# Twelve output products in two bursts of six, and a higher limit for fourth blocks, in a two-sided attention kernel

## The chip, the cores and the metric

The kernel runs on one core of a Trainium2 chip. The metric is the device time of one execution in microseconds; the kernel before takes 1789.94 us, the median of three runs (1789.69 to 1790.98).

## What is computed

Two attention layers read the same input x (2048 x 512) and are mixed row by row. Side A is full softmax attention with 32 heads of 16; side B is softmax attention inside four segments of 512 rows, with a mask, plus a linear memory of the earlier segments. Cut to what matters:

```
a = softmax(q k^T / 4) v, over all 2048 keys, heads joined, @ a_wo
b = per segment: g * (phi(q) M) / (phi(q) z) + (1 - g) * softmax(q k^T / 4 + mask) v, @ b_wo
    M, z: running sums of phi(k) v and phi(k) over the segments before
out = gate * a + (1 - gate) * b,   gate = sigmoid(sum(x * gate_w))
```

## The kernel before

A first phase projects x to q, k and v of both sides and stores them in HBM; it also runs the first 96 row-maximum products. Then comes the main loop, lines 993 to 1025, in which the order of the work is written out by hand: one pass is a slot n, 2368 of them.

A **unit** is a side, a group of four heads and a segment of 512 query rows: 32 units of side A with 64 slots each, 32 of side B with 10. They alternate A, B, A, B (line 102), so a pair takes 74 slots. In one slot the kernel issues

- a score product (`score_part`, line 707): keys by queries into one of three PSUM banks `st`; ACT takes the exponential into a buffer `p` (L745, or L742 for two half pieces of side B). Four slots fill one `p` tile; six such tiles exist (`NP`), and line 716 asserts that the oldest one waiting is still among them. For side B, GpSimd then zeroes the part above the diagonal (L726);
- a row-maximum product for the slot 96 further on (`max_part`, line 214, called with `m = n + LEAD`): queries by keys into one of four PSUM banks `sm`, in rotation, which DVE reduces to one maximum per row (L226 for side A; for side B the masked reduction L238, on one or two parts of the bank). Score and maximum products use the two halves of the rows of the array.

After every third slot (`BURST = 3`) follows one **burst** on PE. It is either P @ V work or work from the list `shared`:

- `some_values` (line 757) takes blocks of 128 keys from `queue` and adds their product with v into the single PSUM bank `ops`; blocks that lie side by side in one `p` tile go into one set of four matmuls, one for each head, at four column positions. How many blocks a burst takes is set by `most` (line 984): three (`MOST`), and a fourth where the queue is longer than a limit that falls from `HIGH` at the unit's first block to `LOW` at its last; near a unit's end the table `ends` (line 982) sets the number. For side B the limit is `LOW` throughout;
- when the last block of a unit is done, ACT copies `ops` to SBUF (L782) and it goes to HBM (L783). From then on the twelve products of `output` (line 911) may be due: half of the products of a block of 128 rows of an earlier segment, the attention of four groups of heads as high and low parts times the output weights, added up in `ops`; ACT copies the sum out (`keep`, L929, or `leave`, L933). The dictionary `between` (lines 942 to 944) says after which units of side A this happens: those of the segments 1 to 3 but for the last two. After the units of side A of segment 0 the twelve products of `later_tile` (line 639) follow in the same way; they are projections of q that the first phase left out;
- while `shared` has anything, a burst takes four pieces of it, so the twelve products fill three bursts, and P @ V waits for that long.

In the last 96 slots (`wide`, line 702) there are no maximum products left; bursts come after six slots and take up to eight blocks. The octets (line 813) scale the raw results on GpSimd at set numbers of slots after a unit's end. DMAs are issued by SP.

Of the kernel before, what the change touches and what calls it, by code (L numbers as in the profile page):

```python
# [26 lines left out]
NO = 4  # L27
# [8 lines left out]
BURST = 3  # L36
LATER = (2, 3)
MOST = 3
LOW, HIGH = 6, 14
NP = 6  # L40
GAP = {"A": 2, "B": 5}
LATE_T = 9
# [5 lines left out]
def gated_mix(ctx, tc, x, xT, wqkv, a_wo, b_wq, b_wk, b_wv, b_wo, beta, gate_w, out):  # L48
# [88 lines left out]
    def raw(t):  # L137

        return t[:].bitcast(F32)
# [109 lines left out]
    def run_todo(m):  # L249

        for e in [e for e in todo if e[0] <= m]:
            todo.remove(e)
            e[1]()
# [359 lines left out]
    def load_halves(key, tag, src, os, n, ns):  # L613

        k = {}

        def load():
            if os[0] == 0:
                halved[key] = wo.tile([128, NO, 2, D], F32R, tag=tag, name="w" + tag)
            if len(os) == 2:  # L620
                t = fr.tile([128, 2, 2, 2, 128], F32R, tag="blk", name="wraws", bufs=2)
                k["t"] = raw(t).rearrange("p k o h t -> p k (o h t)")
            else:
                k["t"] = fr.tile([128, D], F32, tag="res", name="wraw", bufs=2).unsqueeze(1)
            nc.sync.dma_start(k["t"], src[128 * os[0]:128 * os[-1] + 128].rearrange("(k p) d -> p k d", p=128))

        def split(i, o):
            h = halved[key][:, o]
            nc.gpsimd.tensor_copy(h[:, 0], k["t"][:, i])
            nc.gpsimd.tensor_sub(h[:, 1], k["t"][:, i], h[:, 0].bitcast(F32))  # L630
            ready.add((key, o))
        at(n, load)
        for i, o in enumerate(os):
            at(ns[i], lambda i=i, o=o: split(i, o))

    def x_later(c):
        return xT[:, c * CH:(c + 1) * CH]

    def later_tile(c, o):

        def done():
            full = fr.tile([128, CH], F32, tag="part", name="full")
            nc.scalar.copy(full, ops)
            t = fr.tile([128, 2, 2, 2, 128], F32R, tag="blk", name="qhalves", bufs=2)
            t = t.rearrange("p a o h t -> p a (o h t)")
            nc.gpsimd.tensor_copy(t[:, 0], full)
            nc.gpsimd.tensor_sub(t[:, 1], full, t[:, 0].bitcast(F32))
            for i in range(2):
                at(n + 12, lambda i=i: nc.sync.dma_start(
                    qd["A", o, c][16 * i:16 * i + 16].rearrange("d h t -> (d h) t"), raw(t[:, i])))  # L650


            if o == NO - 1 and c == LATER[0]:
                for i in range(2):
                    load_halves(("x", LATER[1]), "B", x_later(LATER[1]), (2 * i, 2 * i + 1), n + 2 + 18 * i,
                                [n + 24 + 29 * i, n + 28 + 29 * i])
            elif o == NO - 1:
                for i, (side, w) in enumerate((("A", a_wo), ("B", b_wo))):
                    load_halves(side, side, w, (0, 1), n + 2 + 18 * i, [n + 22 + 8 * i, n + 26 + 8 * i])
                    for k in range(2, 4):  # L660
                        load_halves(side, side, w, (k,), n + 50 + 22 * i + 3 * (k - 2), [n + 62 + 18 * i + 5 * (k - 2)])

        def f(i):
            k, (a, b) = i // 3, ((1, 0), (0, 1), (0, 0))[i % 3]
            assert {("q", k), (("x", c), k)} <= ready
            nc.tensor.matmul(ops, halved["q"][:, k, a, o * 128:(o + 1) * 128], halved["x", c][:, k, b],  # L666
                             start=(i == 0), stop=(i == 11))
            if i == 11:
                done()
        for i in range(12):  # L670
            yield lambda i=i: f(i)
# [85 lines left out]
    def some_values(n, most):  # L757

        while queue and most and queue[0][0] <= n:
            _, u, i = queue.pop(0)  # L760
            most -= 1
            side, g, c = u
            w = 1
            while (queue and most and queue[0][0] <= n and queue[0][1] == u and (i + w) // 4 == i // 4
                   and (side == "A" or PIECES[i + w][0] == PIECES[i][0])):
                queue.pop(0)
                most -= 1
                w += 1
            p = pt_[u, i // 4]
            if side == "A":  # L770
                c0 = q0 = 128 * (i % 4)
                v = vt[u][:, i // 16, i // 4 % 4]
            else:
                b, c0, q0 = PIECES[i]
                v = vt[u][:, b]
            done = i + w == SLOTS[side]
            for h in range(4):
                nc.tensor.matmul(ops[32 * h:32 * h + 17, q0:q0 + 128 * w], v[:, 17 * h:17 * h + 17], p[:, h, c0:c0 + 128 * w],  # L778
                                 start=(i == 0), stop=done, tile_position=(0, 32 * h))
            if done:  # L780
                raw = ob.tile([128, CH], F32, tag="o", name="oraw")
                nc.scalar.copy(raw, ops)  # L782
                nc.sync.dma_start(od[side, c][4 * g:4 * g + 4].rearrange("h r t -> (h r) t"), raw)  # L783
                stored.add(u)
                if side == "B" and c and g % 2 == 0:
                    octet("M", g // 2, c, n + 4)
                if (side, g ^ 1, c) in stored and u != ("A", NG - 1, NCH - 1):
                    octet(side, g // 2, c, n + (20 if side == "B" and (g < 5 or c < last) else 8))
                if u in between:
                    shared.extend(output(*between[u]))  # L790
                if side == "A" and c == 0:
                    shared.extend(later_tile(LATER[g // NO], g % NO))
                return


# [14 lines left out]
    def at(n, f):  # L810
        beside.setdefault(n, []).append(f)
# [73 lines left out]
    def products(ps, t, b, side, o, start, stop):  # L885

        assert (side, o) in ready
        for i, (x, w) in enumerate(((1, 0), (0, 1), (0, 0))):
            yield lambda i=i, x=x, w=w: nc.tensor.matmul(ps, t[:, b, x], halved[side][:, o, w], start=start and i == 0,  # L889
                                                         stop=stop and i == 2)  # L890
# [3 lines left out]

    fill = []
    shared = []

    blocks = []

# [11 lines left out]
    def output(c, b, pairs, then, ps=ops):  # L911

        ks = [(os, o, i) for os in pairs for o in os for i in range(2)]
        for k in ks:
            def f(n, k=k):
                os, o, i = k
                assert loaded_blocks[c, b, os] > len(blocks) - 2
                t = blocks[loaded_blocks[c, b, os] - 1][:, i, o % 2].unsqueeze(1)
                list(products(ps, t, 0, "AB"[i], o, k == ks[0], k == ks[-1]))[n]()
                if k == ks[-1] and n == 2:  # L920
                    then(ps, c, b)
            for n in range(3):
                yield lambda n=n, f=f: f(n)
# [18 lines left out]
    between = {("A", g, c): (c - 1, g // 2, pairs[g % 2:g % 2 + 1], (keep, leave)[g % 2]) for c in range(1, NCH) for g in range(NG)}  # L942
# [51 lines left out]
    n = 0  # L994
    while n < nS or queue or beside or filled[0] < len(fill):
        for f in beside.pop(n, []):
            f()
        if n < nS:
            score_part(n)
        m = n + LEAD  # L1000
        if m < nS:
            loads(m + PRE)

            max_part(m, lambda: banks[m % 4])
        run_todo(m)
        if n >= nS or n % (2 * BURST if n in wide else BURST) == (2 * BURST if n in wide else BURST) - 1:
            if shared:
                for _ in range(4):
                    shared.pop(0)()
            else:  # L1010
                some_values(n, 8 if n >= nS or n in wide else most())
            if n < 5:


                for i in range(4):
                    nc.tensor.matmul(ops[:, 128 * i:128 * i + 128], identf, identf, start=True, stop=True)
            if any(e[0] < m + 1 for e in late):
                run_late(st_ps, "st", m + 1)
            else:
                for _ in range(0 if n >= nS and queue else 4):  # L1020
                    if filled[0] == len(fill) or fill[filled[0]][0] > n:
                        break
                    fill[filled[0]][1]()
                    filled[0] += 1
        n += 1
# [45 lines left out]
```

## Time and profile before

| | |
|---|---|
| median of three runs | 1789.94 us |
| profiled execution, its own time | 1790.66 us |
| its span | 1788.9 us |
| granted TensorE clock, mean | 0.999 |
| PE, DVE, ACT, POOL busy, share of the span | 99%, 88%, 81%, 36% |
| DMA, mean rate | 146 GB/s |

The profile comes from one execution. A row of a group gives line, engine, operation, tiles (out<-in), shapes and count, then busy time, the mean duration of one in ns, and the idle time of the engine before them. A row of a time line gives the start (us from the span's start), the duration of a run of like instructions from the first start to the last end, and their count; an idle time before it stands in brackets with what ended it. Instructions of one engine overlap: DVE's reduction is on record for 684 ns, yet the next one can start before it ends, so starts are compared with starts. Matmul ends are modelled.

### The profile page before, as it was taken

How to read it: one execution, taken by the hardware profiler on the slowest of the kernel's cores; microseconds unless marked ns; L12 is line 12 of the kernel's file. 1: busy time of each engine (PE TensorE's matmuls, PEld its weight loads, DVE VectorE, ACT ScalarE, POOL GpSimd, SP SyncE). 2: the span in 40 equal slices, each digit the busy share in tenths (PEclk: the TensorE clock that was granted, in tenths of full speed). 3: DMA queues.
4: the chain of work that ended last, by engine and by line, in shares of the span. 5: the costliest groups of instructions: out<-in, count | busy, mean ns of one | idle time of the engine just before them, and what ended most of it. 6: DMA issues, size and time to landing. Idle time of an engine off the chain costs nothing.

```text
span 1788.9 us, 42232 instructions
## 1 busy us (share of the span) xinstructions
PE 1776.2 (99%) x15729; PEld 937.9 (52%) x15729; DVE 1570.5 (88%) x3325; ACT 1443.8 (81%) x2758; POOL 640.7 (36%) x748
## 2 busy tenths in 40 slices
PE   9999999999999999999999999999999999999998
PEld 7887776444444444444444444444444444444444
DVE  4235777999999999999999999999999999999920
ACT  5455444888888888888888888888888888888894
POOL 3002222414161416443434334343425252525442
PEclk9999999999999999999999999999999999999999
DMA  7667555435364446545444545464555444444541
GB/s 234 214 232 235 190 195 191 132 95 147 106 163 114 129 119 172 154 126 147 131 137 124 145 127 145 128 145 127 145 127 132 127 137 126 138 132 123 148 148 61
DMA packets 142284, 261.65 MB, mean 146 GB/s; under 512 B 36312, under 2 KB 60408, under 8 KB 141568
## 3 DMA queue, kind: packets, MB, share of 16 engines
q1 hardware_dynamic: 140576, 257.29, 49.5%
q8 instruction: 125, 2.05, 0.5%
q0 software_dynamic: 1216, 1.14, 0.2%
q14 instruction: 79, 0.65, 0.1%
q10 hardware_dynamic: 288, 0.52, 0.1%
HBM read 174.39 MB, written 83.25 MB: 144 GB/s over the span
## 4 chain that ended last, share of the span: by engine, by line
PE 94%; ACT 2%; DVE 1%; DMA 1%; POOL 1%; issue 0%; SPq 0%; POOLq 0%; ACTq 0%; DVEq 0%
PE ops L778 33%; PE st L722 27%; PE sm L205 14%; PE pr L314 11%; PE ops L889 4%; PE sm L889 2%; PE ops L666 2%; ACT p L745 1%; POOL mn L374 1%; PE num L496 1%; DMA raw<-xT 0%; DMA qdB<-q 0%; PE mt_ps L196 0%; DMA raw<-wqkv 0%; ACT ex L381 0%
## 5 line engine op out<-in xcount | busy, mean ns | idle before, releaser
L745 ACT ACTIVATE p<-st 128x512 f32<-128x512 f32 x2261 | 1191.0, 601 | 148.8 <-PE sm L205 93.1
L226 DVE TENSOR_REDUCE pm<-sm 128x1 f32<-128x512 f32 x2048 | 1282.0, 684 | 12.8 <-PE sm L205 11.5
L722 PE MATMUL st<-qA,kA 50*128 50x512 f32 x2014 | 663.0, 432 | 0.3 <-ACT p L745 0.3
L205 PE MATMUL sm<-kA,qA 48*128 48x512 f32 x2048 | 662.4, 430 | 0.2 <-DVE pm L238 0.2
L778 PE MATMUL ops<-p,vA 128*17 128x256 f32 (+3 forms) x7216 | 556.5, 412 | 0.0
L722 PEld LDWEIGHTS st<-qA,kA 50*128 50x128 f32 x2014 | 327.2, 185 | 390.6 <-ACT p L745 343.4
L205 PEld LDWEIGHTS sm<-kA,qA 48*128 48x128 f32 x2048 | 330.1, 185 | 16.6 <-issue 7.1
L778 PEld LDWEIGHTS ops<-p,vA 128*17 128x17 f32 x7216 | 149.8, 96 | 225.6 <-issue 181.0
L839 POOL TENSOR_TENSOR rcp<-rec,minus 128x32 f32<-128x32 f32 x43 | 234.2, 5447 | 83.2 <-DMA rec<-dend 80.3
L238 DVE CUSTOM_DVE_ANT_0 rest<-sm,mask 128x128 f32<-128x128 f32 (+3 forms) x512 | 247.8, 484 | 3.4 <-PE sm L205 2.2
L726 POOL TENSOR_SCALAR_AFFINE_SELECT p<-p 128x512 f32<-128x512 f32 x128 | 79.4, 636 | 290.0 <-ACT p L745 284.9
L205 PE MATMUL sm<-kB,qB 48*128 48x128 f32 (+3 forms) x512 | 166.3, 385 | 0.0
L722 PE MATMUL st<-qB,kB 50*128 50x512 f32 (+1 forms) x495 | 114.5, 332 | 0.3 <-ACT mt L199 0.3
L377 DVE TENSOR_TENSOR q<-full,q 128x512 fp32r<-128x512 f32 x56 | 38.9, 695 | 72.8 <-ACT q L370 72.7
L722 PEld LDWEIGHTS st<-qB,kB 50*128 50x128 f32 x495 | 72.3, 186 | 56.4 <-ACT p L745 48.6
L187 POOL CAST ms<-nm 128x16 fp32r<-128x16 f32 x32 | 6.7, 209 | 248.6 <-DVE nm L183 248.6
L778 PE MATMUL ops<-p,vB 128*17 128x128 f32 (+3 forms) x1504 | 87.5, 350 | 0.3 <-ACT part L929 0.2
L205 PEld LDWEIGHTS sm<-kB,qB 48*128 48x128 f32 x512 | 80.0, 184 | 0.0
L374 POOL TENSOR_SCALAR mn<-full 128x512 f32<-128x512 f32 x24 | 35.7, 1488 | 103.6 <-ACT full L369 83.3
L369 ACT COPY full<-pr 128x512 f32<-128x512 f32 x56 | 32.6, 582 | 41.0 <-PE pr L314 40.7
L187 POOL CAST ms<-pm 128x16 fp32r<-128x16 f32 x32 | 6.3, 197 | 138.6 <-DVE pm L238 138.6
L835 DVE RECIPROCAL rec<-rec 128x32 f32<-128x32 f32 x1 | 0.4, 353 | 60.3 <-DMA rec<-odA 60.3
(187 smaller groups left out, 1673.1 us busy)
## 6 DMA issues: line engine op xcount, KB each, us to landing
kA<-kdA SPq DMA_DIRECT2D x256, 128.0 KB
vA<-vdA SPq DMA_DIRECT2D x31, 544.0 KB
kA<-kdA SPq DMA_DIRECT2D x256, 64.0 KB
kdA<-q SPq DMA_DIRECT2D x32, 256.0 KB
qdB<-q SPq DMA_DIRECT2D x32, 256.0 KB
qA<-qdA SPq DMA_DIRECT2D x64, 128.0 KB
kdB<-q SPq DMA_DIRECT2D x32, 256.0 KB
qB<-qdB SPq DMA_DIRECT2D x64, 128.0 KB
```

The lines of the kernel that those rows point to most:

```text
L205: nc.tensor.matmul(ps[:, n0:n0 + n], rows(qt[u][:, :, s * 128:(s + 1) * 128], h, 48), rows(k[:, :, k0:k0 + n], h, 48), start=True, stop=True)
L226: nc.vector.tensor_reduce(pm[:, h, s, kc:kc + 1], ps, axis=AX.X, op=ALU.max)
L238: rows_left.append(lambda h=h, s=s, n0=n0, w=w: nc.vector.tensor_tensor_reduce(out=tri["rest"][:, 0:w], in0=ps[:, n0:n0 + w], in1=tri["mas ...
L314: nc.tensor.matmul(ps, l(a, k), r(b, k), start=(n == 0), stop=(n == 11))
L374: nc.gpsimd.tensor_scalar_min(ph["mn"], full, 0.0)
L377: nc.vector.tensor_sub(q2, full, q1.bitcast(F32))
L722: nc.tensor.matmul(ps[:, n0:n0 + CH - q0], rows(k[:, :, b * 128:(b + 1) * 128], h, 50), rows(q[:, :, q0:], h, 50), start=True, stop=True)
L726: nc.gpsimd.affine_select(out=x, in_=x, pattern=[[0, 4], [1, 128]], base=0, channel_multiplier=-1, compare_op=ALU.is_ge, fill=0.0)
L745: nc.scalar.activation(p[:, h], ps, AF.Exp, scale=SCALE)
L778: nc.tensor.matmul(ops[32 * h:32 * h + 17, q0:q0 + 128 * w], v[:, 17 * h:17 * h + 17], p[:, h, c0:c0 + 128 * w], start=(i == 0), stop=done ...
L839: eng.tensor_tensor(r, rec, minus, op=ALU.pow)
L889: yield lambda i=i, x=x, w=w: nc.tensor.matmul(ps, t[:, b, x], halved[side][:, o, w], start=start and i == 0, stop=stop and i == 2)
```

## The change

Three things differ. The list `shared` now holds bursts, that is lists of pieces, and a burst on PE issues one such list. The twelve products of `output` are cut into two lists of six; those of `later_tile` into three of four, as they were. And `HIGH`, the limit on the queue at a unit's first block, is 18 in place of 14. Every product is issued as before, in the same order among themselves.

```diff
-LOW, HIGH = 6, 14
+LOW, HIGH = 6, 18
...
                 if u in between:
-                    shared.extend(output(*between[u]))
+                    shared.extend(runs(output(*between[u]), 6))
                 if side == "A" and c == 0:
-                    shared.extend(later_tile(LATER[g // NO], g % NO))
+                    shared.extend(runs(later_tile(LATER[g // NO], g % NO), 4))
...
+    def runs(pieces, n):
+        pieces = list(pieces)
+        return [pieces[i:i + n] for i in range(0, len(pieces), n)]
+
...
             if shared:
-                for _ in range(4):
-                    shared.pop(0)()
+                for f in shared.pop(0):
+                    f()
```

## The prediction

> **What bounds the kernel now.** I read the page first, then the busy times of the engines by stretch, then the time lines of PE and DVE around the places where output products are issued.
>
> ```profile
> span 1788.9 us, 42232 instructions
> PE 1776.2 (99%) x15729; PEld 937.9 (52%) x15729; DVE 1570.5 (88%) x3325; ACT 1443.8 (81%) x2758; POOL 640.7 (36%) x748
> L226 DVE TENSOR_REDUCE pm<-sm 128x1 f32<-128x512 f32 x2048 | 1282.0, 684 | 12.8 <-PE sm L205 11.5
> ```
>
> ```profile
> 340.00:1710.00 1370.00, 1369.79 (x13597) 656.50 (x13591) 1365.42 (x2932) 1213.17 (x2342) 539.01 (x623) 1.00 0.48 133
> 1712.00:1788.00 76.00, 71.77 (x453) 36.46 (x449) 3.97 (x9) 50.59 (x102) 26.30 (x29) 0.99 0.34 110
> ```
>
> The columns of the stretches are length, then busy time of PE, PEld, DVE, ACT, POOL. From 340 to 1710 us PE and DVE are both full: 1369.8 and 1365.4 of 1370 us; ACT has 11% left. After 1712 DVE is nearly empty, because the last 96 slots have no maximum ahead of them. PE's figure counts modelled, overlapping ends, so I ask which of the two waits. The Trainium skill's page "Perfetto Trace Analysis", section "Identifying the Most-Contended Engine", says the same from the other side: occupancy is a fair measure for the Vector engine and a bad one for matmuls; these rows cannot prove it for PE, but they agree for DVE.
>
> The main loop makes three slots, then one burst on PE; I call this a round. DVE's own pace in a round comes from stretches in which it does not wait:
>
> ```profile
> 1004.57 4.87 DVE L226 TENSOR_REDUCE pm<-sm 128x1 f32<-128x512 f32 x8
> 1009.36 0.68 DVE L238 CUSTOM_DVE_ANT_0 rest<-sm,mask 128x512 f32<-128x512 f32 x1
> ...
> 1701.04 0.28 DVE L238 CUSTOM_DVE_ANT_0 rest<-sm,mask 128x128 f32<-128x128 f32 x1
> ...
> 1702.32 0.69 DVE L226 TENSOR_REDUCE pm<-sm 128x1 f32<-128x512 f32 x1
> 1702.92 0.68 DVE L238 CUSTOM_DVE_ANT_0 rest<-sm,mask 128x512 f32<-128x512 f32 x1
> ```
>
> Eight reductions from start to start take 1009.36 - 1004.57 = 4.79 us, 0.60 each: 1.80 us a round. A round with one two-part maximum of side B (two masked reductions of 128 and 384 columns, two plain ones) takes 1702.92 - 1701.04 = 1.88 us. PE's pace in a round is the distance between the first products of two rounds. The first group of outputs that I took:
>
> ```profile
> 1035.95 0.50 PE L205 MATMUL sm<-kA,qA 48*128 48x512 f32 x1
> ...
> 1036.90 0.96 PE L889 MATMUL ops<-wA,blk 128*128 128x512 f32 x3
> 1037.70 0.40 PE L889 MATMUL ops<-wB,blk 128*128 128x512 f32 x1
> ...
> 1038.04 0.55 PE L205 MATMUL sm<-kB,qB 48*128 48x128 f32 x2
> ...
> 1040.12 0.55 PE L205 MATMUL sm<-kB,qB 48*128 48x128 f32 x2
> ...
> 1041.40 0.86 PE L889 MATMUL ops<-wB,blk 128*128 128x512 f32 x3
> ...
> 1042.19 0.73 PE L205 MATMUL sm<-kA,qA 48*128 48x512 f32 x2
> ...
> 1043.87 0.72 PE L205 MATMUL sm<-kA,qA 48*128 48x512 f32 x2
> ```
>
> A round with four output products takes 2.09, 2.08 and 2.07 us; the next, with three blocks of P @ V, 1043.87 - 1042.19 = 1.68. Four blocks cost 1.89 (below). So PE is faster than DVE in a round of three blocks (by 0.12), slower in a round of four (by 0.09), and slower by 0.28 in a round of four output products (by 0.20 where DVE has its 1.88). DVE sets the pace over the whole stretch and stands still only where PE falls behind; a standstill of DVE is never made good, since DVE has no spare time. What DVE lost in three successive kinds of group:
>
> ```profile
> 1034.37 4.28 DVE L226 TENSOR_REDUCE pm<-sm 128x1 f32<-128x512 f32 x7
> 1038.62 0.29 DVE L238 CUSTOM_DVE_ANT_0 rest<-sm,mask 128x128 f32<-128x128 f32 x1
> ...
> 1042.06 4.38 DVE L226 TENSOR_REDUCE pm<-sm 128x1 f32<-128x512 f32 x7
> 1046.35 0.68 DVE L238 CUSTOM_DVE_ANT_0 rest<-sm,mask 128x512 f32<-128x512 f32 x1
> ```
>
> ```profile
> 989.81 4.48 DVE L226 TENSOR_REDUCE pm<-sm 128x1 f32<-128x512 f32 x7
> 994.54 0.29 DVE L238 CUSTOM_DVE_ANT_0 rest<-sm,mask 128x128 f32<-128x128 f32 x1 [0.25 <-PE sm L205]
> ...
> 1002.16 0.68 DVE L238 CUSTOM_DVE_ANT_0 rest<-sm,mask 128x512 f32<-128x512 f32 x1
> ```
>
> ```profile
> 1080.47 4.27 DVE L226 TENSOR_REDUCE pm<-sm 128x1 f32<-128x512 f32 x7
> ...
> 1092.27 0.68 DVE L238 CUSTOM_DVE_ANT_0 rest<-sm,mask 128x512 f32<-128x512 f32 x1
> ```
>
> Each of the three stretches holds the same work: 14 plain reductions (14 x 0.60 = 8.39 from 4.79 / 8) and the seven pieces between them (1.88 + 1702.32 - 1701.04 = 3.16), together 11.55 us. They took 11.98, 12.35 and 11.80: lost 0.43, 0.80 and 0.25, on average 0.49 us a group. Lines 942 to 944 make 24 - 2 = 22 groups: 10.9 us now.
>
> **The change part by part.** *Output bursts.* Twelve products a group come as six and six. The second half of a burst of four gives the price of one more product: (0.86 - 0.40) / 2 = 0.23 us from the rows of 1041.40 (three) and 1037.70 (one). Two more make a round 2.08 + 0.46 = 2.54 us. Against DVE's 1.80 in the first and 1.88 in the second round PE falls behind by 0.74 + 0.66 = 1.40 us a group; the third round is now one of three blocks, in which PE gains.
>
> What DVE can ride over is the lead: how long a product has been finished when DVE takes it. In the first group the product of 1035.95 is finished at 1036.45 and taken at 1034.37 + 4 x 0.60 = 1036.77: 0.32 us. Where DVE waits, hardly anything is left of it:
>
> ```profile
> 993.95 0.55 PE L205 MATMUL sm<-kB,qB 48*128 48x128 f32 x2
> ```
>
> finished 994.50, taken 994.54 after an idle 0.25: 0.04. The lead on entering a group comes from the unit's last bursts. I followed the planner's count (lines 982 to 991 and 1006 to 1011) slot by slot with old and new numbers, counting blocks only. Its check is a row of the groups by line and shape:
>
> ```profile
> L778 PE MATMUL ops<-p,vA 128*17 128x512 f32 x976 | 127.1, 598 | 0.0
> ```
>
> The old numbers give just these 976 matmuls of 512 columns. They end the units with 3, 4 and 1 blocks in turn, the new ones with 3, 3 and 4. The 0.32 belongs to a unit that ends with 3; a fourth block takes 0.21 (1.89 - 1.68) from it: 0.32, 0.32, 0.11, mean 0.25, of which 0.21 can be used. DVE then loses 1.40 - 0.21 = 1.19 us a group, 0.70 more than now: 22 x 0.70 = **+15.4 us**. Bounds: with no lead 1.40, +20.0; with the lead that a unit ending in one block would leave (0.32 + 2 x 0.21 = 0.74, 0.70 usable) 0.70, +4.6. I take the middle one since its row is of a unit that ends as two of the three new ones do.
>
> *Fourth blocks.* By the count, bursts of four fall from 291 to 200, bursts of three rise from 364 to 488, single blocks fall from 12 to 1; output bursts go from 66 to 44, the 24 bursts of later_tile stay as they are. What four blocks cost now, where they come straight after a group:
>
> ```profile
> 1094.37 1.05 PE L778 MATMUL ops<-p,vA 128*17 128x512 f32 x8
> ...
> 1096.26 1.05 PE L778 MATMUL ops<-p,vA 128*17 128x512 f32 x8
> ```
>
> ```profile
> 1094.68 5.00 DVE L226 TENSOR_REDUCE pm<-sm 128x1 f32<-128x512 f32 x8
> 1099.61 0.68 DVE L238 CUSTOM_DVE_ANT_0 rest<-sm,mask 128x512 f32<-128x512 f32 x1
> ```
>
> The round takes 1.89 us; DVE's eight reductions take 4.93 instead of 4.79: 0.14 lost. The new limit 18 puts threes there in the units that I followed, so this goes. It happens in about one unit of three, some 0.2 us in each with what follows: 10 x 0.2 = **-2 us**; bounds 0 (the loss only moves to where the fours now stand) and -4 (twice the seen loss).
>
> *Cut of the blocks.* The same blocks of P @ V are cut otherwise: 9144 matmuls by the count in place of 8720. An unsplit three and a split one:
>
> ```profile
> 1002.34 0.84 PE L778 MATMUL ops<-p,vA 128*17 128x384 f32 x8
> ...
> 1003.11 0.50 PE L722 MATMUL st<-qA,kA 50*128 50x512 f32 x1
> ...
> 1004.12 0.84 PE L778 MATMUL ops<-p,vA 128*17 128x128 f32 x16
> ...
> 1004.89 0.50 PE L722 MATMUL st<-qA,kA 50*128 50x512 f32 x1
> ```
>
> Both take 0.77 us up to the next score, so the cut costs 0. The Trainium skill's page "Perfetto Trace Analysis", section "Matmuls", holds that larger matmuls are more efficient than smaller ones. It speaks against the change; at these widths the two rows do not bear it out, and by the rows the sum stays as it is.
>
> *The rest at nothing.* The copies out of ops (L782, L929, L933) keep their number and stand behind the same bursts; three score slots (0.95 us, 1035.95 to 1036.90) cover them, and without that cover each would cost one copy. No DMA is added; those at a unit's end (raw result, octet loads) move by at most a few slots on SP. The products' block is loaded 20 slots before the unit's end as now. ACT needs 1213 of 1370 us and only starves longer in a burst of six. Side B's P @ V starts a round (1.8 us) earlier in most units and needs GpSimd's diagonal; in the first group above it is done well ahead of it:
>
> ```profile
> 1039.78 0.63 POOL L726 TENSOR_SCALAR_AFFINE_SELECT p<-p 128x512 f32<-128x512 f32 x1 [0.34 <-ACT p L742]
> ```
>
> It ends at 1040.41, the first block that could need it starts after 1042.19. In the tail one burst (slot 2279) has seven blocks and not four, 3 x 0.21 = 0.64 us of PE, partly beside ACT: between 0 and 0.6, taken as **+0.3**.
>
> Sum: 15.4 - 2 + 0.3 = +13.7 us. On the profiled execution, 1790.66 us (1788.9 of it span), that is 1804.4; the median 1789.94 is 0.7 lower, so **1803.6 us**.
>
> **The rivals.** *A, PE sets the pace.* PE's 99.98% in the main stretch speaks for it, DVE's lack of idle time against it. Then only PE's sum counts: 44 x 2.54 - 66 x 2.08 + 124 x 1.68 - 91 x 1.89 - 11 x 1.26 = -3.1 us, as fewer bursts of outputs and fours are paid for by more threes: 1786.8 us, the case on the other side. It decides if DVE's losses in a round of six stay at those of a round of four. The Trainium skill's page "TensorEngine Tiling (Array Packing)", section "Key Properties", has a change of tiling mode drain the engine; the count of bursts, and so of such changes, stays the same here, and by that rule nothing is won or lost.
>
> *B, the lead is longer.* Runs of threes fill it before every group (for: 0.12 us gained in each such round; against: only four sm banks, and the lead of 0.32 was seen after threes). +4.6 - 2 + 0.3 gives 1792.8 us.
>
> *C, no lead, and the fours lose as much as before:* +20.0 + 0 + 0.6 gives 1810.5 us.
>
> *D, GpSimd is late* with a diagonal because a reciprocal power of some 5 us (L839) moved ahead of it; it would cost a few us once or twice: 1809 us. Nothing in the rows points to it, beyond the shift of the octets.
>
> That the change does not do what it says can be left out: the pieces are plain lists of six.
>
> **How the numbers follow.** A measurement of this kernel tells 0.2% (3.6 us) from no change. My case has 74%, A 6%, B 8%, C 9%, D 3%. A lies within 0.2% but close to faster, B within 0.2%, the rest is slower: faster 4%, same 10%, slower 86%. The range 1796 to 1811 takes in the upper bound and most of the lower, and leaves out A and the better half of B.
>
> **What would show it.** In the profile after, DVE should lose some 1.2 us in each such stretch of 11.55 us (about 12.7 long), with an idle gap before a reduction behind each burst of six; rounds with six products should take 2.5 us, those with three blocks 1.68 to 1.80. DVE's runs after a group should show 0.60 a reduction. I am wrong if the stretches with six products last 12 us or less, if rounds of six take under 2.4 us, or if PE's time line has gaps at B's P @ V.

## The result, and the profile after

The changed kernel takes **1804.03 us**, the median of six runs (1803.44 to 1805.8), against 1789.82 us for six runs of the kernel before beside it (1788.9 to 1790.98). The ratio is 1.008, with a 95% interval of 1.0067 to 1.0093: the change costs 14.2 us. The prediction was 1803.6.

First the page of the kernel after, its span and busy times, then its main stretch, with the columns of the prediction's fence.

```profile
span 1801.7 us, 43085 instructions
PE 1791.0 (99%) x16153; PEld 974.1 (54%) x16153; DVE 1565.9 (87%) x3325; ACT 1443.5 (80%) x2758; POOL 641.3 (36%) x748
```

```profile
340.00:1710.00 1370.00, 1370.00 (x13848) 685.46 (x13844) 1346.82 (x2895) 1200.85 (x2320) 534.53 (x615) 1.00 0.47 132
```

In the same 1370 us DVE now has 1346.82 us of busy time, 18.6 less than before; PE shows the full share in both. To see where the time went I took two of the small reductions of L183, which close the maxima of a unit of side A, as marks: the first that falls in the main loop (one more, at 274.5 us before, still belongs to the first phase) and the last. First the two marks in the time line of DVE before, then those after.

```profile
336.20 0.21 DVE L183 TENSOR_REDUCE nm<-pm 128x16 f32<-128x64 f32 x1
...
1710.87 0.22 DVE L183 TENSOR_REDUCE nm<-pm 128x16 f32<-128x64 f32 x1
```

```profile
334.38 0.22 DVE L183 TENSOR_REDUCE nm<-pm 128x16 f32<-128x64 f32 x1
...
1722.96 0.22 DVE L183 TENSOR_REDUCE nm<-pm 128x16 f32<-128x64 f32 x1
```

Between the marks lie 1374.67 us before and 1388.58 after: +13.9. After the last mark follow 78.0 us up to the end of the span before and 78.7 after: +0.7. The first mark comes 1.8 us earlier in this execution of the kernel after, and so does the reduction in the first phase (272.6 against 274.5), where the code is unchanged; that is why the two spans differ by 12.8 only.

Inside the stage, on PE, the group of outputs that the prediction took first (start, duration, then engine, line and count):

```profile
1037.93 0.50 PE L205 MATMUL sm<-kA,qA 48*128 48x512 f32 x1
...
1038.88 0.96 PE L889 MATMUL ops<-wA,blk 128*128 128x512 f32 x3
1039.68 0.87 PE L889 MATMUL ops<-wB,blk 128*128 128x512 f32 x3
...
1040.48 0.55 PE L205 MATMUL sm<-kB,qB 48*128 48x128 f32 x2
...
1043.02 0.55 PE L205 MATMUL sm<-kB,qB 48*128 48x128 f32 x2
...
1044.74 0.50 PE L205 MATMUL sm<-kA,qA 48*128 48x512 f32 x1
```

The two rounds of six take 2.55 and 2.54 us, the third, now of three blocks, 1.72. The same place on DVE, then the two other kinds of group:

```profile
1036.13 4.27 DVE L226 TENSOR_REDUCE pm<-sm 128x1 f32<-128x512 f32 x7
1041.07 0.29 DVE L238 CUSTOM_DVE_ANT_0 rest<-sm,mask 128x128 f32<-128x128 f32 x1 [0.68 <-PE sm L205]
...
1041.35 0.69 DVE L226 TENSOR_REDUCE pm<-sm 128x1 f32<-128x512 f32 x1
...
1043.61 0.29 DVE L238 CUSTOM_DVE_ANT_0 rest<-sm,mask 128x128 f32<-128x128 f32 x1 [0.49 <-PE sm L205]
...
1043.88 0.69 DVE L226 TENSOR_REDUCE pm<-sm 128x1 f32<-128x512 f32 x1
...
1049.14 0.68 DVE L238 CUSTOM_DVE_ANT_0 rest<-sm,mask 128x512 f32<-128x512 f32 x1
```

```profile
991.08 4.26 DVE L226 TENSOR_REDUCE pm<-sm 128x1 f32<-128x512 f32 x7
...
1003.85 0.68 DVE L238 CUSTOM_DVE_ANT_0 rest<-sm,mask 128x512 f32<-128x512 f32 x1
...
1083.16 4.26 DVE L226 TENSOR_REDUCE pm<-sm 128x1 f32<-128x512 f32 x7
...
1095.94 0.68 DVE L238 CUSTOM_DVE_ANT_0 rest<-sm,mask 128x512 f32<-128x512 f32 x1
...
1098.36 4.87 DVE L226 TENSOR_REDUCE pm<-sm 128x1 f32<-128x512 f32 x8
1103.14 0.68 DVE L238 CUSTOM_DVE_ANT_0 rest<-sm,mask 128x512 f32<-128x512 f32 x1
```

The stretches that hold 11.55 us of work take 13.01, 12.77 and 12.78 us: DVE loses 1.46, 1.22 and 1.23 in a group. Behind each burst of six stands the idle gap, ended by the product of L205 that came too late. The list of waits has the sum of them (total us, times, longest); first the row of the kernel before, then of the kernel after:

```profile
DVE rest L238 <- PE sm L205: 2.2, 9, 0.3
```

```profile
DVE rest L238 <- PE sm L205: 22.7, 46, 0.7
```

The wait falls on the masked piece that opens a round. The eight reductions behind the third kind of group, which lost 0.14 us before, take 1103.14 - 1098.36 = 4.78 us, so nothing is lost there any more.

I then did the same for every round of the stage: the distance between DVE's starts in successive rounds, less DVE's own pace for that content (1.80 us for three plain reductions, the like for rounds with masked ones). The 22 groups of outputs lost 11.2 us before and 28.8 after (1.31 each); the rounds of P @ V lost 3.3 before and nothing after (-0.3, against a pace that is a mean); the groups of `later_tile` 3.4 and 3.9. Differences: +17.6, -3.6 and +0.5, together +14.5 against the stage's +13.9; the paces are means, and the 0.6 left over is within what they leave open. These sums are used below for the other kernels too, as "lost by DVE".

### The profile page after: what moved, and what is told of

Read it like the earlier page. It is cut to its first block, busy times and chain, and to the rows that moved or that the text cites. A ratio compares the mean times of both kernels' runs of the same rounds, so it can differ in the third digit from the quotient of the medians.

```text
span 1801.7 us, 43085 instructions
## 1 busy us (share of the span) xinstructions
PE 1791.0 (99%) x16153; PEld 974.1 (54%) x16153; DVE 1565.9 (87%) x3325; ACT 1443.5 (80%) x2758; POOL 641.3 (36%) x748
## 4 chain that ended last, share of the span: by engine, by line
PE 93%; ACT 2%; DVE 2%; DMA 2%; POOL 1%; issue 0%; SPq 0%; POOLq 0%; DVEq 0%; ACTq 0%
PE ops L778 33%; PE st L722 27%; PE sm L205 15%; PE pr L314 10%; PE ops L889 4%; PE sm L889 2%; PE ops L666 1%; POOL mn L374 1%; ACT p L745 1%; DVE pm L226 1%; PE num L496 0%; DMA vs<-wqkv 0%; DMA qdA<-q 0%; ACT ex L381 0%; DVE q L377 0%
## 5 line engine op out<-in xcount | busy, mean ns | idle before, releaser
L205 PE MATMUL sm<-kA,qA 48*128 48x512 f32 x2048 | 679.7, 438 | 0.1
L778 PE MATMUL ops<-p,vA 128*17 128x128 f32 (+3 forms) x7640 | 560.7, 398 | 0.0
L205 PEld LDWEIGHTS sm<-kA,qA 48*128 48x128 f32 x2048 | 330.3, 184 | 21.8 <-issue 7.1
L778 PEld LDWEIGHTS ops<-p,vA 128*17 128x17 f32 x7640 | 159.2, 96 | 225.6 <-issue 181.9
L205 PE MATMUL sm<-kB,qB 48*128 48x128 f32 (+3 forms) x512 | 166.1, 384 | 0.0
L205 PEld LDWEIGHTS sm<-kB,qB 48*128 48x128 f32 x512 | 79.9, 184 | 0.0
```

What stands on the lines that cost most here:

```text
L205: nc.tensor.matmul(ps[:, n0:n0 + n], rows(qt[u][:, :, s * 128:(s + 1) * 128], h, 48), rows(k[:, :, k0:k0 + n], h, 48), start=True, stop=True)
```

## Experiments

Each kernel ran beside the kernel before on the same chip, whose median was 1790.0 to 1790.5 us; ratios are to it.

**Is it DVE's waiting, or PE's work?** In two kernels the reductions of side A read half the columns, so that DVE has time to spare (their maxima leave out half of the keys); the rest of the one is the kernel before, of the other the kernel after.

```diff
-            nc.vector.tensor_reduce(pm[:, h, s, kc:kc + 1], ps, axis=AX.X, op=ALU.max)
+            nc.vector.tensor_reduce(pm[:, h, s, kc:kc + 1], ps[:, 0:256], axis=AX.X, op=ALU.max)
```

> The kernel before, but side A's maxima are taken over 256 of the 512 columns of each product, so that DVE's reduction gets shorter by some 0.27 us and DVE no longer sets the pace. PE issues what it did. Theory: PE sets the pace; its rounds sum to 66 x 2.08 + 24 x 2.07 + 291 x 1.89 + 364 x 1.68 + 12 x 1.26 = 1364 us in place of some 1382: about 1772 us. Rival (PE was the bound all along): 1790 us.

> The changed kernel with side A's maxima over 256 of 512 columns. Theory: with DVE out of the way the bursts of six cost nothing but PE's sum, which is 3 us smaller than that of the kernel before: between 4 us faster than the kernel before with the same cut and equal to it, about 1769 us. Rival (the 14 us come from PE, ACT, GpSimd or DMA): 14 us slower than the kernel before with the same cut.

Measured: 1775.2 us (1773.8 to 1775.88) and 1772.28 us (1771.78 to 1773.39), both some 3 us above what was expected, with the expected distance between them. The main stretch of the kernel before with half reductions, then that of the kernel after with them:

```profile
340.00:1690.00 1350.00, 1349.79 (x13511) 638.84 (x13504) 910.52 (x2913) 1205.68 (x2329) 537.40 (x619) 1.00 0.49 135
```

```profile
340.00:1690.00 1350.00, 1350.00 (x13948) 652.18 (x13945) 911.66 (x2919) 1207.98 (x2333) 537.76 (x622) 1.00 0.49 135
```

With DVE at 911 of 1350 us the change costs nothing; it gains 2.9 us, and rival A's sum over PE's bursts was -3.1. So the difference in PE's sum fits, and what the change costs, it costs by making DVE wait: with DVE relieved the loss is gone. The rows also show how little PE's busy time tells: it is full in these kernels as in the kernel after, which takes 32 us more. That agrees with the section "Identifying the Most-Contended Engine" of the Trainium skill's page "Perfetto Trace Analysis", by which matmul occupancy is a bad measure; no number here rests on it.

**How does the loss go with the length of a burst?** One burst of twelve, and four bursts of three. Since P @ V waits for four bursts with threes, a seventh `p` tile holds what waits; a kernel with fours and seven tiles tells what that tile does alone.

```diff
-                    shared.extend(runs(output(*between[u]), 6))
+                    shared.extend(runs(output(*between[u]), 12))
```

> All twelve products in one burst, limit HIGH 18. Theory: a round with twelve products takes 2.08 + 8 x 0.23 = 3.92 us on PE, DVE 1.80, 0.21 us of lead helps: 1.91 us lost in a group, 42 us in all in place of 10.9, less 3 for the fours: +28 us, 1818 us. Rival (PE's sum): 22 x 3.92 - 66 x 2.08 + 211 x 1.68 - 156 x 1.89 - 11 x 1.26 = -5 us, 1785 us. Second rival (each burst has a fixed price and its length none): fewer bursts of outputs, so below the changed kernel.

```diff
-NP = 6
+NP = 7
...
-                    shared.extend(runs(output(*between[u]), 6))
+                    shared.extend(runs(output(*between[u]), 3))
```

> Output products in four bursts of three, limit HIGH 18, and seven buffers p in place of six, since P @ V waits a round longer. Theory: a round with three products takes 2.08 - 0.23 = 1.85 us on PE, so DVE falls short by 0.05 in a round at its 1.80 and by nothing at 1.88: the groups lose next to nothing in place of 10.9 us; 66 more bursts of four than with three bursts of four products give back up to 66 x 0.09 = 6 us: 1779 to 1786 us, faster than both kernels. Rival (what counts is how long P @ V waits, not the length of a burst): slower than before.

The kernel before with limit and tile:

```diff
-LOW, HIGH = 6, 14
-NP = 6
+LOW, HIGH = 6, 18
+NP = 7
```

> The kernel before with limit HIGH 18 and seven buffers p, output products in three bursts of four: what the seventh buffer does by itself beside the kernel with four bursts of three. Theory (the length of the bursts decides): as with limit 18 and six buffers, 1787 to 1790 us, 4 to 5 us above the kernel with bursts of three. Rival (the seventh buffer gives the gain): about 1784 us.

| products in a burst (limit 18) | median us | ratio, 95% | lost by DVE in a group, us |
|---|---|---|---|
| 3, seven tiles | 1784.11 | 0.9969 (0.9957 to 0.998) | 0.04 |
| 4, seven tiles | 1788.71 | 0.9992 (0.9983 to 1.0001) | 0.50 |
| 6 (the change, run again) | 1804.7 | 1.008 (1.0067 to 1.0092) | 1.31 |
| 12 | 1820.2 | 1.0166 (1.0152 to 1.018) | 2.05 |

Twelve products on PE and the DVE stretch around them, in the kernel with one burst:

```profile
1043.34 0.50 PE L205 MATMUL sm<-kA,qA 48*128 48x512 f32 x1
...
1047.29 0.55 PE L205 MATMUL sm<-kB,qB 48*128 48x128 f32 x2
```

```profile
1041.55 4.27 DVE L226 TENSOR_REDUCE pm<-sm 128x1 f32<-128x512 f32 x7
...
1047.88 0.29 DVE L238 CUSTOM_DVE_ANT_0 rest<-sm,mask 128x128 f32<-128x128 f32 x1 [2.06 <-PE sm L205]
...
1055.30 0.68 DVE L238 CUSTOM_DVE_ANT_0 rest<-sm,mask 128x512 f32<-128x512 f32 x1
```

The round takes 3.95 us; 2.08 + 8 x 0.23 = 3.92 by the prediction's price of a product. DVE stands still once, for 2.06 us, and loses 13.75 - 11.55 = 2.20. Now the kernel with threes:

```profile
1031.86 0.50 PE L205 MATMUL sm<-kA,qA 48*128 48x512 f32 x1
...
1033.70 0.55 PE L205 MATMUL sm<-kB,qB 48*128 48x128 f32 x2
...
1035.55 0.55 PE L205 MATMUL sm<-kB,qB 48*128 48x128 f32 x2
```

```profile
1030.06 4.27 DVE L226 TENSOR_REDUCE pm<-sm 128x1 f32<-128x512 f32 x7
...
1041.71 0.68 DVE L238 CUSTOM_DVE_ANT_0 rest<-sm,mask 128x512 f32<-128x512 f32 x1
```

A round of three products takes 1.84 and 1.85 us, within 0.05 of DVE's 1.80 to 1.88; DVE loses 0.10 here, and 0.8 us in all groups together. This kernel is **6.2 us faster than the kernel before**, and it does the same twelve products, in twice as many bursts as the changed one. The seventh tile isn't what does it: fours with seven tiles can't be told from the time before. Of the some 10 us that the groups lose less than in the kernel with fours and seven tiles, the rounds of P @ V take some 7 back, as the planner's count has 66 more bursts of four blocks.

With `later_tile` cut into threes too:

```diff
-                    shared.extend(runs(later_tile(LATER[g // NO], g % NO), 4))
+                    shared.extend(runs(later_tile(LATER[g // NO], g % NO), 3))
```

> As the kernel with four bursts of three output products, seven buffers p and limit HIGH 18, and the twelve products of later_tile in four bursts of three as well. Theory: the 3.9 us that DVE loses in the eight groups of later_tile go too, 24 more bursts of four give back up to 2: 2 to 4 us below the kernel with three output products alone, 1776 to 1783 us. Rival: no difference between the two.

1784.88 us, ratio 0.9971 (0.9961 to 0.9982): no further gain, where 2 to 4 us were expected. The groups of `later_tile` lose 0.3 us and not 3.8, but the rounds of P @ V lose 4.1 more: what waits through one more burst comes back as fourth blocks.

**What does the limit do by itself?** The kernel before with 18 (`four_high18`), and the kernel after with 14, run twice:

```diff
-LOW, HIGH = 6, 18
+LOW, HIGH = 6, 14
```

> Output products in three bursts of four as before, limit HIGH 18. Theory: only the losses of DVE in rounds of four blocks at a unit's beginning go, -2 to -3.5 us: 1786.5 to 1788 us. Rival (the limit has part in the slowdown): slower than before by over 1 us.

> Output products in two bursts of six, limit HIGH left at 14. Theory (DVE sets the pace and loses 1.2 us in a group with bursts of six, 0.5 now): 22 x 0.7 = +15 us, without the 2 to 3 us that the higher limit saves: 1804 to 1807 us. Rival (PE's sum counts): 44 x 2.54 - 66 x 2.08 + 88 x 1.68 - 66 x 1.89 = -2.4 us, 1787 us.

> Output products in two bursts of six, limit HIGH 14, beside the changed kernel. Theory: 1 to 2 us below the changed kernel. Rival: 1 to 2 us above it.

> The changed kernel once more, beside the kernel with bursts of six and the old limit 14 on the same chip. Theory: 1803 to 1805 us, and 1 to 2 us above the one with limit 14, because limit 18 ends the units with 3, 3 and 4 blocks in place of 3, 4 and 1, so that the products enter a group with 0.32, 0.32 and 0.10 us of lead in place of 0.32, 0.20 and 0.75. Rival (the limit saves the same 1.4 us as with bursts of four, and the distance seen lay in the chip): 1 to 2 us below it.

| | limit 14 | limit 18 |
|---|---|---|
| bursts of four | 1 (the kernel before) | 0.9992 (0.9983 to 1.0001) |
| bursts of six | 1.0066 (1.0053 to 1.008), again 1.0069 (1.0056 to 1.0081) | 1.008 (1.0067 to 1.0092) |

With fours the higher limit saves 1.4 us, less than was expected, and that can't be told from nothing. With sixes it costs 2.2 us (1804.7 against 1802.47 on one chip), and the kernel with limit 14 is faster than the 1804 to 1807 us expected of it. The traces show two parts of the turn. The limit also sets how many blocks stand at a unit's end, and so the lead on entering a group: with sixes DVE loses 27.5 us in the groups at 14 and 28.8 at 18, while with fours the groups lose the same at both. And in the rounds of P @ V the higher limit saves some 2.8 us with fours, but with sixes, which have fewer bursts of four blocks to begin with (225 against 291 by the planner's count), only some 0.4. In the traces the stage with sixes is 1.2 us longer at 18; where the rest of the 2.2 lies stays open.

**Is a longer lead worth anything?** The table `ends` was rewritten so that units end with ever fewer blocks, which lets PE get ahead before a group, and `LOW` went from 6 to 3 with it; once with fours, once with sixes.

```diff
-LOW, HIGH = 6, 18
+LOW, HIGH = 3, 18
...
-    ends = {"A": {9: 3, 8: 4, 7: 3, 6: 3, 5: 5}, "B": {10: 3, 7: 3, 4: 4}}
+    ends = {"A": {9: 4, 8: 4, 7: 3, 6: 3, 5: 4, 4: 3, 3: 2, 2: 1}, "B": {10: 3, 7: 3, 4: 4}}
```

> Output products in three bursts of four, limits LOW 3 and HIGH 18, and the table of ends set so that every unit of side A ends with a burst of one block. Theory (the lead on entering a group decides): a group loses 0.25 us as those behind a one-block end do now, not 0.49: -5 us, and -2 to -3 us for the higher limit, some of it given back by 37 more bursts of four: 1781 to 1786 us, faster than both kernels. Rival (the lead has no part): as with the higher limit alone, 1787 us, or slower for the fours.

> Output products in two bursts of six, limits LOW 3 and HIGH 18, every unit of side A ending with a burst of one block. Theory (the lead decides): shortfall 1.40 us a group less a usable lead of 0.70: 0.70 lost, 15.4 in place of 10.9: +4.5 us, less 2 to 3.5 for the limit: 1790 to 1793 us, 11 us below the changed kernel by the table of ends alone. Rival (the lead has no part): as the changed kernel, 1804 us.

Both were misses: 1792.91 us, 1.0015 (1.0007 to 1.0024), and 1805.93 us, 1.0089 (1.0075 to 1.0103). The lead was there, but it bought little. PE and ACT in the group at the same place of the kernel with fours and these ends, then DVE:

```profile
1035.63 0.50 PE L205 MATMUL sm<-kA,qA 48*128 48x512 f32 x1
...
1036.06 0.49 PE L205 MATMUL sm<-kA,qA 48*128 48x512 f32 x1
...
1036.55 0.49 PE L205 MATMUL sm<-kA,qA 48*128 48x512 f32 x1
...
1038.15 0.38 PE L722 MATMUL st<-qB,kB 50*128 50x256 f32 x1
```

```profile
1034.92 1.57 ACT L745 ACTIVATE p<-st 128x512 f32<-128x512 f32 x3 [0.36 <-PE sm L205]
1036.37 0.60 ACT L782 COPY oraw<-ops 128x512 f32<-128x512 f32 x1
1036.83 1.62 ACT L745 ACTIVATE p<-st 128x512 f32<-128x512 f32 x3
```

```profile
1034.32 4.31 DVE L226 TENSOR_REDUCE pm<-sm 128x1 f32<-128x512 f32 x7
...
1046.48 0.68 DVE L238 CUSTOM_DVE_ANT_0 rest<-sm,mask 128x512 f32<-128x512 f32 x1
```

The product of 1035.63 ends at 1036.13 and is taken at 1034.32 + 4 x 0.60 = 1036.72: a lead of 0.59 us, where it was 0.32. Yet the stretch takes 12.16 us, a loss of 0.61, more than the 0.43 before. PE's first round takes 1038.15 - 1035.63 = 2.52 us with only four outputs, because its three products stand 0.43 and 0.49 us apart. In the kernel before they stand 0.33 and 0.25 apart at this place, where the product of 1035.95 (in the prediction's rows) is followed by these:

```profile
1036.28 0.44 PE L205 MATMUL sm<-kA,qA 48*128 48x512 f32 x1
...
1036.53 0.44 PE L205 MATMUL sm<-kA,qA 48*128 48x512 f32 x1
```

The distances fit ACT's: its three exponentials of 1034.92 each record some 0.60 us, about 0.48 apart, so they end near 1035.5, 1036.0 and 1036.5, and each score of this round needs the `st` bank that one of them frees. The three pairs of score and maximum product start within 0.1 us behind those ends (1035.63, 1036.06, 1036.55). So a PE that comes earlier meets ACT. This is the worst of the three kinds of group: the one that lost 0.80 loses 0.28 now. Over the whole stage the groups lose 8.9 us with these ends and not 11.2, while the rounds of P @ V lose some 4.6 us more than in the kernel before. By the trace that loss lies in the middle of the units of side A, not at their ends: the 208 rounds of four blocks with 11 to 44 blocks left lose 7.6 us, the 29 with ten or fewer 0.5. The lower `LOW` lets a fourth block in sooner there, but no run changes `LOW` alone. That ACT sets the three distances is read off the rows; no run took its wait away alone.

With sixes it is the same. PE, then DVE, in the group at that place of the kernel with sixes and these ends:

```profile
1040.13 0.50 PE L205 MATMUL sm<-kA,qA 48*128 48x512 f32 x1
```

```profile
1038.82 4.31 DVE L226 TENSOR_REDUCE pm<-sm 128x1 f32<-128x512 f32 x7
1043.70 0.29 DVE L238 CUSTOM_DVE_ANT_0 rest<-sm,mask 128x128 f32<-128x128 f32 x1 [0.58 <-PE sm L205]
...
1046.24 0.29 DVE L238 CUSTOM_DVE_ANT_0 rest<-sm,mask 128x128 f32<-128x128 f32 x1 [0.49 <-PE sm L205]
```

The product of 1040.13 ends at 1040.63 and is taken at 1038.82 + 4 x 0.60 = 1041.22, again a lead of 0.59. The first round still takes DVE 1043.70 - 1041.22 = 2.48 us, the second 2.54. Over the stage a group loses 1.20 us in place of 1.31.

## Why the prediction was right, point by point

*The bound.* DVE sets the pace and doesn't make good a standstill. Shown: with DVE relieved the change gains 2.9 us, with DVE full it costs 14.2. Rival A's sum is the right one for PE and decides only in the first case.

*The price of a product and of a round.* 0.23 us a product gave 2.54; measured 2.55 and 2.54, and 3.95 for twelve (3.92 by that price).

*The lead.* Predicted 0.32, 0.32 and 0.11 in some order. In the group above the product of 1037.93 ends at 1038.43 and is taken at 1036.13 + 4 x 0.60 = 1038.53: 0.10; by the same working the other two groups have 0.32. Rival B's longer lead isn't there, nor is rival C's none. `six_ends1` shows besides that B's price was wrong: with leads of 0.59 us and more before every group, a group still loses 1.20 us, and not 0.70. A lead of 0.75 does occur, in the kernel before behind the units that end with one block (a product that starts at 1081.62, ends at 1082.12 and is taken at 1080.47 + 4 x 0.60 = 1082.87), as the prediction had worked out with 0.74.

*The loss in a group.* Predicted 1.19, measured 1.31 on average: mis-sized by 0.12, or 2.6 us over 22 groups; against the loss before (11.2, predicted 10.9) the term came out at +17.6 and not +15.4. Part of it is in the rows. After each wait DVE takes the short piece of 128 columns, and its next reduction starts 0.28 or 0.27 us later (1041.07 to 1041.35, 1043.61 to 1043.88). Where DVE doesn't wait, it is 0.20 later, as in this row of the kernel before, which follows the piece of 1701.04:

```profile
1701.24 0.69 DVE L226 TENSOR_REDUCE pm<-sm 128x1 f32<-128x512 f32 x1
```

Behind the first wait this is taken up by the next, since PE sets the length of that round; behind the second it comes on top, 0.07 us a group, which the sum did not have. Why the reduction starts later there no run shows. The rest lies in the first round. PE falls behind by 0.74 there; DVE loses 0.51 of it in the 15 groups with a lead of 0.32, and all 0.74 in the 7 with 0.10. So the lead was worth 0.16 us on average and not 0.21.

*The fourth blocks.* Predicted -2 (0 to -4), in the trace -3.6: mis-sized the other way. The loss lay where the prediction had it: the rounds of four blocks at the beginnings of side A's units (over 44 blocks left) lost 3.7 us before and nothing after, the seen 0.14 behind the groups among them. But the prediction put the saving down to the limit, and that is only half of it. With sixes at limit 14 these rounds lose 1.2 us, so the bursts of six alone bring most of the saving; with fours the limit brings it.

*The cut of the blocks* cost nothing that can be seen: the after_half kernel has all of it and is faster. *The tail* took +0.7 and not +0.3. GpSimd was not late: all waits of P @ V for its results come to 2.4 us before and 3.3 after over the whole span, so rival D is out.

The sum of the stage and the tail, 13.9 + 0.7 = 14.6, stands against 13.7 predicted. That the total came out within 0.5 us owes something to luck: +2.2 in the groups and -1.6 in the fours nearly cancel.

## What to carry to other kernels

When a full engine is fed by another that is only slightly faster, it isn't the amount of side work on the feeder that costs, but the longest stretch of it without food for the other: cut it into pieces that keep each round at the consumer's pace, even if that makes more bursts (here three products, 1.85 us, against a pace of 1.80 to 1.88). Before counting on a lead, see how much of it reaches the wait: here leads of 0.6 us and more before every group lowered its loss from 1.31 to 1.20 us, and a PE made to come earlier met ACT. Fewer, longer bursts pay only where the consumer has time to spare, and a run in which it is relieved tells in one look which case it is.

## What the runs showed that I had not expected

The shortest bursts left the stage 1703.07 - 334.39 = 1368.7 us long, by the marks of L183 in the kernel with threes:

```profile
334.39 0.20 DVE L183 TENSOR_REDUCE nm<-pm 128x16 f32<-128x64 f32 x1
...
1703.07 0.22 DVE L183 TENSOR_REDUCE nm<-pm 128x16 f32<-128x64 f32 x1
```

With half reductions, where PE is bound by DVE no more, the changed kernel's stage is 1359.4 us by the same marks. So a kernel with DVE relieved of a third of its work is only 9 us shorter in this stage than one that does all of it with short bursts: the two engines stand so close together that relieving one of them gains little before the other sets the pace. Threes and half reductions together were not run.
